# A retention layer feeding a bilinear feed-forward: the opening in another order, w_out in three loads, small TensorE bursts at other places

## The chip, the cores and the metric

The kernel runs on one core of one Trainium2 chip. A core has TensorE (matrix products, into the accumulation memory PSUM), VectorE, ScalarE and GpSimd (elementwise work; GpSimd also issues most loads here), and SyncE, which issues stores and transposing transfers. Each engine takes its own instructions in the order in which the program gives them. Sixteen DMA engines move data between the chip's memory and the on-chip buffer. The metric is the device time of one execution in microseconds (us); the time of a kernel is the median of its runs.

## The reference

Eight batches, eight heads, 576 positions, head size 64. First an attention without softmax, whose scores decay with distance by a factor per head; then a feed-forward whose two inner products are multiplied with each other:

```python
scores = (1 / sqrt(64)) * q @ k.T                       # per batch and head
gamma  = 1 - 2.0 ** (-5 - head)
ret    = scores * where(row >= col, gamma ** (row - col), 0)
x      = (ret @ v), heads side by side                  # 4608 tokens x 512
out    = ((x @ w_a) * (x @ w_b)) @ w_out                # 512 -> 1536 -> 512
```

Inputs and output are float32; the kernel computes in bf16 with float32 sums.

## The kernel before, in words

**Attention in chunks.** The decay is split into a factor on v and k's side (a table `vs`, by position) and one on the output side (a table `qs`), so that the scores need only a triangular mask. A chunk is 128 tokens, a step 64; a running state (the sum of k·v over the steps so far) replaces the scores with earlier steps. `load` (loads of q, k and v, cast to bf16 for q and k, issued by GpSimd), `vscale` (v times its table), `transposes` (q and k of a chunk turned by TensorE, or by a transposing transfer from SyncE), `kv` (the step sums, TensorE, with the additions on VectorE and the bf16 copies of the states on ScalarE put into a list `later`), `stage1` (products with states, then scores, then the masks on VectorE) and `stage2` (scores times v, the rest of the state products, and the writing of x, transposed, by VectorE) handle chunks; a unit is two chunks. Chunks 0 to 3 are taken as two "fresh" units, 0 and 1, of 256 tokens each, by functions of their own (`fresh_...`). These work with one running sum, `kv_sum`.

**Feed-forward in blocks.** A block is 512 tokens. `ffn_ab` makes, for each of 12 columns F of 128, four products with w_a (`pa`), a copy to bf16 by ScalarE (`ha`), four products with w_b (`pb`), and the product of both by VectorE (`hT`). `ffn_out` makes the output of 128 tokens at a time in 12 products with w_out (`po`), copied out by ScalarE and VectorE in turn and stored by SyncE. Both are generators: after each product they yield its cost in units of one 512-column product and whether other work may be put in there. `pop()` at their edges runs one entry of `later`.

**What sets the order.** Every engine's order is written out by hand. The opening is straight code: idle products that keep TensorE going while the first loads come, then the fresh units mixed with the first three columns of block 0. After it, `run` walks the generators and adds up the cost in `at`; the list `todo` holds (position, function, arguments), and at the first edge at or past a position the function is called, so that its instructions stand there in each engine's order. Block 0's columns 3 to 11 take positions 24 to 96, its output 96 to 144; block 1's two halves 144 to 192 and 192 to 240, its output 240 to 288; each later block 144. `first(g)` is `flush` (all of `later`) and `stage1` of unit g; for g from 2 on it also calls the transposing transfers and `vscale` of unit g+2 and the loads of unit g+3. `second(g)` is `flush`, `stage2`, and for g from 2 on `kv` of unit g+2.

**PSUM.** Eight banks in three pools: `ps_ffn` (tag "ab", 4 banks; `pa`, `pb`, `po`, `kv_sum` and some transposes), `ps_o` (2 banks; attention outputs), `ps_x` (2 banks; scores and step sums).

**Loads.** GpSimd issues them in the program's order: unit 0, unit 1, w_a and w_b in pieces by columns (`load_w`, two transfers for each of the two), then all of w_out in one transfer (`load_wo`, line 124), then chunks 4 to 9. Between w_b's columns up to 384 and w_a's from 384 on, GpSimd scales v of unit 1 (`fresh_vscale`, line 479).

The lines that the profile names most: `pa` 414, `ha` 419, `pb` 422, `hT` 427, `po` 453, its copies 462 and 464; transposes 275 and their copies 277 and 278; step sums 294; state products 339, scores 359, masks 367, scores times v 381, x 398; loads of q and k 102, v 110, w_a and w_b 118; `qs` pieces 235. In the opening: idle products 596, transposes 492, copies of the turned q and k 614 to 630, scores 549, masks 561, k·v sums 514 and their bf16 copies 521, state products 527, scores times v 572, x 583 to 588, and 601, `settled`, one small product that reads the last state before the last products of a unit are begun (the probe).

Of the kernel before, what the change touches and what calls it, by code (L numbers as in the profile page):

```python
# [18 lines left out]
def kernel(  # L19
# [240 lines left out]
            op=ALU.mult)  # L260
        vb_of[i] = vb

    def transposes(i, by_dma):
# [8 lines left out]
        tp = ps_ffn.tile([128, 2, HP, 128], BF16, tag="ab", name="tp")  # L272
        for w in (0, 1):
            for p in range(HP):
                nc.tensor.transpose(tp[:, w, p, :],  # L275
                                    qk[:, w, p * 128:(p + 1) * 128], identity)
        nc.scalar.copy(qkT[:, 0], tp[:, 0])
        nc.vector.tensor_copy(qkT[:, 1], tp[:, 1])
# [126 lines left out]
    def ffn_ab(blk, tok0, n, f0, f1):  # L405
# [4 lines left out]
        for F in range(f0, f1):  # L410
# [18 lines left out]
            pop()  # L429
            yield n / 512, True  # L430

    def ffn_out(blk):
        hT = hT_of.pop(blk)
        for u in range(4):
            tok = 512 * blk + 128 * u
            if tok + 128 == NTOK:
                for c0, w, eng, copy in (
                        (0, 320, nc.sync, nc.vector.tensor_copy),
                        (320, 192, nc.scalar, nc.scalar.copy)):
                    pl = ps_ffn.tile([128, 512], FP32, tag="ab", name="po")  # L440
                    for F in range(NF):
                        nc.tensor.matmul(pl[:, 0:w],  # L442
                                         hT[:, F, u * 128:(u + 1) * 128],
                                         wo_sb[:, F, c0:c0 + w],
                                         start=(F == 0), stop=(F == NF - 1))
                        yield w / 512, False
                    osb = o_pool.tile([128, DM], FP32, tag="osb", name="osb")
                    copy(osb[:, 0:w], pl[:, 0:w])
                    eng.dma_start(out[tok:tok + 128, c0:c0 + w], osb[:, 0:w])
                continue  # L450
            po = ps_ffn.tile([128, 512], FP32, tag="ab", name="po")
            for F in range(NF):
                nc.tensor.matmul(po, hT[:, F, u * 128:(u + 1) * 128],  # L453
                                 wo_sb[:, F, :],
                                 start=(F == 0), stop=(F == NF - 1))
# [4 lines left out]
            osb = o_pool.tile([128, DM], FP32, tag="osb", name="osb")  # L460
            if u % 2 == 0:
                nc.scalar.copy(osb, po)  # L462
            else:
                nc.vector.tensor_copy(osb, po)  # L464
            nc.sync.dma_start(out[tok:tok + 128, :], osb)
# [5 lines left out]
    fresh_state = {0: zero_state}  # L471
    fv, fT, fo, fsT = {}, {}, {}, {}

    def fresh_vscale(u, h0, h1, eng):
        if u not in fv:
            fv[u] = [vb_pool.tile([128, DM], BF16, tag="vb", name="fvb")
                     for _ in (0, 1)]
        for e in (0, 1):
            eng.tensor_tensor(  # L479
                fv[u][e].rearrange("p (h d) -> p h d", h=H)[:, h0:h1, :],  # L480
                vf2[:, u, :].rearrange("p (h e d) -> p h e d", h=H, e=2)[
                    :, h0:h1, e, :],
                vs_all[:, 2 * e + u, h0:h1].unsqueeze(2).to_broadcast(
                    [128, h1 - h0, D]), op=ALU.mult)
# [47 lines left out]
    def fresh_state1(u):  # L532
# [2 lines left out]
                 for s in (0, 1)]  # L535
        for j in (0, 2):
            for h, s in ((j, 1), (j + 4, 1), (j + 1, 0), (j + 5, 0)):
                fresh_from_state(u, h, s, j == 0)

    def fresh_scores(u, places):  # L540
        qT, kT = fT[u]
# [24 lines left out]
    def fresh_stage2(u):  # L566
        for j in (0, 2, 1, 3):
            for e in (0, 1):
                for s in (0, 1):
                    for c in (0, 1):  # L570
# [5 lines left out]
                            start=False, stop=True, skip_group_check=True)  # L576
        for j in (0, 2):
            for h, s in ((j, 0), (j + 4, 0), (j + 1, 1), (j + 5, 1)):
                fresh_from_state(u, h, s, False)
        for s in (0, 1):  # L580
            t0 = 256 * u + 128 * s
            if u == 1:
# [16 lines left out]
    def settled(u, n=1, w=128):  # L599
        for _ in range(n):  # L600
# [13 lines left out]
    nc.vector.tensor_tensor(q_out, tq.rearrange("p c e t -> p c t e"),  # L614
                            qs0.rearrange("p c (t e) -> p c t e", e=2),
                            op=ALU.mult)
    nc.scalar.copy(k_out[:, 0:2], tk[0])
    nc.vector.tensor_copy(k_out[:, 2:4], tk[1])
    make_qs(256, 512)
    idle_products(2)  # L620
    fresh_vscale(0, 4, 8, nc.vector)
    fresh_scores(0, (X, AB))
    fresh_kv(0, 0)
    q_out, k_out = fresh_tiles(1)
    tq = fresh_transposed(1, 0, 0, HP, AB)
    nc.scalar.copy(q_out, tq.rearrange("p c e t -> p c t e"))
    tk = fresh_transposed(1, 1, 0, HP, AB)
    fresh_state1(0)
    fresh_kv(0, 1)
    nc.scalar.copy(k_out, tk)  # L630
    fresh_vscale(1, 0, 8, nc.gpsimd)
    load_w(384, 768)
    ramp(idx[:, 512:S], [[1, S - 512]], 512, 0)
    load_w(768, 1152)
    load_w(1152, DFF)
    settled(0)
    fresh_stage2(0)
    fresh_scores(1, (X, O))
    run_all(ffn_ab(0, 0, 256, 0, 1))
    fresh_kv(1, 0)  # L640
    fresh_state1(1)
    fresh_kv(1, 1)
    state_of[8] = fresh_state[4]
    run_all(ffn_ab(0, 0, 256, 1, 2))
    settled(1)
    fresh_stage2(1)
    run_all(ffn_ab(0, 0, 256, 2, NF1))
    run_all(ffn_ab(0, 256, 256, 0, NF1))
    make_keep()
# [56 lines left out]
    for g in range(3, len(units)):  # L706
# [55 lines left out]
```

## Time and profile before

| | |
|---|---|
| time, median of 11 runs | 336.42 us (335.24 to 340.38) |
| the profiled execution's own time | 336.01 us |
| its span | 334.2 us |
| instructions in it | 8838 |
| VectorE, ScalarE, GpSimd busy | 165.4, 112.5, 143.6 us |
| granted TensorE clock | 1.0 throughout |
| read from and written to the chip's memory | 37.75 MB and 9.44 MB |

The span runs from the first to the last instruction of the profiled execution; the time of a run also has what lies around it. In the rows of a timeline, the first number is the start in us, the second the length; then engine, line, operation and tiles (output <- inputs), the count of instructions merged into the row, and in brackets how long the engine had been idle before it and what ended that. The engine names are PE (TensorE), PEld (its weight loads), DVE (VectorE), ACT (ScalarE), POOL (GpSimd) and SP (SyncE). A row of waits gives who waited for whom, the total, the number of times and the longest. A row of stretches gives the stretch, its length, TensorE's busy time and products, the granted clock, the busy share of the DMA engines and GB/s.

### The profile page before, as it was taken

Reading aid. Unit: us, or ns where it says so; the run is one execution under the profiler, and the core shown is the slowest. Engines: PE = TensorE matmul, PEld = TensorE weight load, DVE = VectorE, ACT = ScalarE, POOL = GpSimd, SP = SyncE. Lnnn points to the kernel's source line nnn. Section 1 sums busy time; section 2 is a strip of 40 time slices with the busy share of each in tenths; the row PEclk is TensorE's granted clock in tenths of the full one; section 3 lists DMA queues with packets and bytes.
Section 4 is the critical chain, followed back from the end, with each engine's and each line's share of the span. In section 5 each row is a group of like instructions: output and inputs, shape, how many; then the busy total and the mean of one; then the engine's idle time right before and its main releaser. Section 6 shows DMA issues by size and latency. Waiting matters only on the chain.

```text
span 334.2 us, 8838 instructions
## 1 busy us (share of the span) xinstructions
PE 323.0 (97%) x3746; PEld 166.6 (50%) x3746; DVE 165.4 (49%) x324; ACT 112.5 (34%) x233; POOL 143.6 (43%) x176
## 2 busy tenths in 40 slices
PE   7889889989999999999999999999999999999995
PEld 3564346868544444445444444454444444444443
DVE  6754346757544555346445644454445534444321
ACT  4737523545143213332332223322323133203321
POOL 8786299698647795308250837072100000000000
PEclk9999999999999999999999999999999999999999
DMA  9999999999999999916999499939900700020002
GB/s 144 201 146 195 212 196 235 184 155 139 193 195 196 126 126 224 168 10 92 108 192 118 78 100 230 101 63 123 196 0 29 132 34 1 13 86 31 2 31 94
DMA packets 116151, 40.94 MB, mean 122 GB/s; under 512 B 102992, under 2 KB 109392, under 8 KB 116112
## 3 DMA queue, kind: packets, MB, share of 16 engines
q0 software_dynamic: 80688, 23.34, 71.6%
q1 hardware_dynamic: 35280, 16.95, 28.4%
q8 instruction: 29, 0.48, 0.6%
q10 hardware_dynamic: 144, 0.10, 0.1%
q14 instruction: 10, 0.08, 0.1%
HBM read 37.75 MB, written 9.44 MB: 141 GB/s over the span
## 4 chain that ended last, share of the span: by engine, by line
PE 85%; DMA 9%; POOL 3%; issue 1%; ACT 1%; DVE 0%; POOLq 0%; ACTq 0%
PE po L453 26%; PE pa L414 25%; PE pb L422 25%; DMA wo_sb<-in_moe_w_out_dram 4%; DMA wa_sb<-in_moe_w_a_dram 2%; PE o L339 2%; PE o L381 2%; DMA fqk<-in_k_dram 2%; PE kv L294 2%; DMA qk<-in_k_dram 1%; PE sc L359 1%; POOL fqk L141 1%; PE po L442 1%; POOL fvb L479 1%; PE tp L275 0%
## 5 line engine op out<-in xcount | busy, mean ns | idle before, releaser
L427 DVE TENSOR_TENSOR hT<-ha,pb 128x512 bf16<-128x512 bf16 (+1 forms) x123 | 76.5, 622 | 100.7 <-PE pb L422 85.6
L414 PE MATMUL pa<-xT,wa_sb 128*128 128x512 bf16 (+1 forms) x492 | 114.0, 354 | 2.2 <-issue 1.6
L422 PE MATMUL pb<-xT,wb_sb 128*128 128x512 bf16 (+1 forms) x492 | 113.5, 353 | 0.0
L419 ACT CAST ha<-pa 128x512 bf16<-128x512 f32 (+1 forms) x123 | 65.6, 533 | 124.7 <-PE pa L414 123.6
L453 PE MATMUL po<-wo_sb,hT 128*128 128x512 bf16 x420 | 95.5, 380 | 0.8 <-DMA wo_sb<-in_moe_w_out_dram 0.8
L422 PEld LDWEIGHTS <-wb_sb 128*128 128x128 bf16 x492 | 48.1, 98 | 45.3 <-issue 0.3
L414 PEld LDWEIGHTS <-wa_sb 128*128 128x128 bf16 x492 | 46.8, 98 | 47.0 <-issue 2.9
L256 POOL TENSOR_TENSOR vb<-vf,vs_all 128x512 bf16<-128x512 f32 x30 | 31.6, 1069 | 78.6 <-PE o L339 44.9
L453 PEld LDWEIGHTS <-hT 128*128 128x128 bf16 x420 | 39.0, 98 | 45.6 <-DMA wo_sb<-in_moe_w_out_dram 1.3
L462 ACT COPY osb<-po 128x512 f32<-128x512 f32 x18 | 10.5, 585 | 74.8 <-PE po L453 74.8
L102 POOL DMA_DIRECT2D qk<-in_q_dram x36 | 31.0, 867 | 6.8 <-DMA wo_sb<-in_moe_w_out_dram 6.2
L110 POOL DMA_DIRECT2D vf<-in_v_dram x36 | 31.9, 888 | 1.4 <-issue 1.1
L102 POOL DMA_DIRECT2D qk<-in_k_dram x36 | 31.2, 875 | 0.6 <-DMA wa_sb<-in_moe_w_a_dram 0.3
L367 DVE TENSOR_TENSOR sT<-sc,keep 128x512 bf16<-128x512 f32 x32 | 20.6, 685 | 12.1 <-PE sc L359 12.1
L398 DVE TENSOR_TENSOR xT<-o,qs 128x512 bf16<-128x512 f32 x32 | 20.6, 685 | 11.8 <-PE o L339 11.7
L307 DVE TENSOR_TENSOR s<-kv,s 128x256 f32<-128x256 f32 x49 | 20.6, 420 | 5.8 <-ACT sbf L317 4.5
L317 ACT CAST sbf<-s 128x256 bf16<-128x256 f32 x56 | 21.1, 406 | 3.1 <-DVE s L305 2.7
L464 DVE COPY osb<-po 128x512 f32<-128x512 f32 x17 | 11.7, 687 | 19.3 <-PE po L453 19.3
L339 PE MATMUL o<-qkT,sbf 64*64 64x64 bf16 x456 | 12.1, 196 | 0.1
L339 PEld LDWEIGHTS <-sbf 64*64 64x64 bf16 x456 | 8.2, 108 | 5.7 <-issue 5.5
L381 PEld LDWEIGHTS <-vb 64*64 64x64 bf16 x512 | 6.4, 108 | 6.6 <-issue 6.6
L381 PE MATMUL o<-sT,vb 64*64 64x64 bf16 x512 | 8.2, 195 | 0.0
(75 smaller groups left out, 128.7 us busy)
## 6 DMA issues: line engine op xcount, KB each, us to landing
out_dram<-osb SPq DMA_DIRECT2D x35, 256.0 KB, 5.1
vf<-in_v_dram POOLq DMA_DIRECT2D x29, 256.0 KB, 6.1
qk<-in_q_dram POOLq DMA_DIRECT2D x28, 128.0 KB, 6.3
qk<-in_k_dram POOLq DMA_DIRECT2D x28, 128.0 KB, 7.0
wo_sb<-in_moe_w_out_dram POOLq DMA_DIRECT2D x1, 1536.0 KB, 14.6
wa_sb<-in_moe_w_a_dram POOLq DMA_DIRECT2D x6, 192.0 KB, 6.5
wb_sb<-in_moe_w_b_dram POOLq DMA_DIRECT2D x6, 192.0 KB, 7.5
vf<-in_v_dram POOLq DMA_DIRECT2D x8, 128.0 KB, 5.9
```

The source lines that it names most:

```text
L102: nc.gpsimd.dma_start(t[r0:r0 + n, w, :].rearrange("p (h d) -> p h d", h=H), src[b, :, s0:s0 + n, :].rearrange("h s d -> s h d"))
L110: nc.gpsimd.dma_start(t[r0:r0 + n, :].rearrange("p (h d) -> p h d", h=H), v[b, :, s0:s0 + n, :].rearrange("h s d -> s h d"))
L256: eng.tensor_tensor(vb.rearrange("p (h d) -> p h d", h=H), vf.rearrange("p (h d) -> p h d", h=H), vs[:, i % PER, :].unsqueeze(2).to_broadc ...
L307: nc.vector.tensor_tensor(new, ps[s][:, ci], last_sum[0], op=ALU.add)
L317: nc.scalar.copy(sb, new)
L339: nc.tensor.matmul(o[s][half(c), ci, j, :], st[half(r), p, :], qkt_of[i][half(r), 0, p, half(s)], start=start, stop=True, skip_group_check ...
L381: nc.tensor.matmul(o[s][half(c), ci, j, :], vb[half(s), 64 * h:64 * h + 64], sT[half(s), h % 2, ci, h // 2, :], start=False, stop=True, sk ...
L414: nc.tensor.matmul(pa[:, 0:n], wa_sb[:, c, fs], xT[:, c, tok0:tok0 + n], start=(c == 0), stop=(c == NC - 1))
L419: nc.scalar.copy(ha[:, 0:n], pa[:, 0:n])
L422: nc.tensor.matmul(pb[:, 0:n], wb_sb[:, c, fs], xT[:, c, tok0:tok0 + n], start=(c == 0), stop=(c == NC - 1))
L427: nc.vector.tensor_tensor(hT[:, F, off:off + n], ha[:, 0:n], pb[:, 0:n], op=ALU.mult)
L453: nc.tensor.matmul(po, hT[:, F, u * 128:(u + 1) * 128], wo_sb[:, F, :], start=(F == 0), stop=(F == NF - 1))
```

## The change

- Unit 0 is carried to its end (states, second k·v sum, last products, x) before k of unit 1 is transposed; before, q and k of unit 1 were transposed in between. Products with the zero state at the beginning of the sequence (8 in all) fall away.
- The copy of unit 1's transposed k is split between ScalarE and VectorE.
- v of unit 1 is scaled on VectorE (even rows, one instruction) and ScalarE (odd rows, one instruction for each head) where GpSimd did both. `load_w(384, 768)` is so right behind its forerunner in GpSimd's order.
- Column 1 of block 0's first half is begun (its four `pa` products) between the two k·v sums of unit 1, and ended after unit 1's last products.
- The four `qs` pieces of unit 1 are put at other places in ScalarE's order.
- w_out comes in three loads of four rows of blocks, with the loads of chunks 4 and 5 between; block 0's output is made in three passes over all four groups of 128 tokens (`ffn_out_parts`), so that each pass needs one third of w_out. Its four stores come in the last pass.
- The transposes of chunks 4 and 5 go to `ps_x`; chunk 4's stand at position 96 (was 112).
- `kv` of units 2 and 3 at 208 and 228 (were 184 and 208), `first` and `second` of unit 2 at 248 and 260 (were 232 and 244), of unit 3 at 272 and 280 (were 260 and 272).

```diff
+    def store(tok, po, u):
...
+    def ffn_out_parts(blk, parts):
+
+        hT = hT_of.pop(blk)
+        po = [ps_ffn.tile([128, 512], FP32, tag="ab", name="po")
+              for _ in range(4)]
+        for f0, f1 in parts:
+            for u in range(4):
+                for F in range(f0, f1):
+                    nc.tensor.matmul(po[u], hT[:, F, u * 128:(u + 1) * 128],
+                                     wo_sb[:, F, :],
+                                     start=(F == 0), stop=(F == NF - 1))
+                    if F < f1 - 1:
+                        yield 1.0, False
+                if f1 == NF:
+                    store(512 * blk + 128 * u, po[u], u)
+                pop()
+                yield 1.0, True
...
-        for e in (0, 1):
+        for e in es:
+            if eng is nc.scalar:
+                for h in range(h0, h1):
+                    nc.scalar.activation(
+                        fv[u][e][:, 64 * h:64 * h + 64],
+                        vf2[:, u, 128 * h + 64 * e:128 * h + 64 * e + 64],
+                        AF.Copy, bias=0.0,
+                        scale=vs_all[:, 2 * e + u, h:h + 1])
+                continue
...
-                fresh_from_state(u, h, s, j == 0)
+                if u or s:
+                    fresh_from_state(u, h, s, j == 0)
...
+    make_qs(256, 512, (0, 1))
     nc.scalar.copy(k_out[:, 0:2], tk[0])
     nc.vector.tensor_copy(k_out[:, 2:4], tk[1])
-    make_qs(256, 512)
+    make_qs(256, 512, (2,))
     idle_products(2)
     fresh_vscale(0, 4, 8, nc.vector)
     fresh_scores(0, (X, AB))
     fresh_kv(0, 0)
+    make_qs(256, 512, (3,))
+    fresh_state1(0)
+    fresh_kv(0, 1)
     q_out, k_out = fresh_tiles(1)
     tq = fresh_transposed(1, 0, 0, HP, AB)
     nc.scalar.copy(q_out, tq.rearrange("p c e t -> p c t e"))
-    tk = fresh_transposed(1, 1, 0, HP, AB)
-    fresh_state1(0)
-    fresh_kv(0, 1)
-    nc.scalar.copy(k_out, tk)
-    fresh_vscale(1, 0, 8, nc.gpsimd)
+    settled(0)
+    fresh_stage2(0)
+    tk = [fresh_transposed(1, 1, 0, 2, AB), fresh_transposed(1, 1, 2, 4, X)]
+    nc.scalar.copy(k_out[:, 0:2], tk[0])
+    nc.vector.tensor_copy(k_out[:, 2:4], tk[1])
     load_w(384, 768)
+    fresh_vscale(1, 0, 8, nc.vector, (0,))
+    fresh_vscale(1, 0, 8, nc.scalar, (1,))
+    fresh_scores(1, (X, O))
+    run_all(ffn_ab(0, 0, 256, 0, 1))
+    fresh_kv(1, 0)
+    begun = ffn_ab(0, 0, 256, 1, 2)
+    for _ in range(NC):
+        next(begun)
+    fresh_state1(1)
+    fresh_kv(1, 1)
+    state_of[8] = fresh_state[4]
     ramp(idx[:, 512:S], [[1, S - 512]], 512, 0)
     load_w(768, 1152)
     load_w(1152, DFF)
-    settled(0)
-    fresh_stage2(0)
-    fresh_scores(1, (X, O))
-    run_all(ffn_ab(0, 0, 256, 0, 1))
-    fresh_kv(1, 0)
-    fresh_state1(1)
-    fresh_kv(1, 1)
-    state_of[8] = fresh_state[4]
-    run_all(ffn_ab(0, 0, 256, 1, 2))
     settled(1)
     fresh_stage2(1)
+    run_all(begun)
     run_all(ffn_ab(0, 0, 256, 2, NF1))
...
-    load_wo(0, NF)
...
-    load(*range(4, 10))
-    todo = [(110, vscale, (4, nc.vector)), (110, vscale, (5, nc.vector)),
-            (110, transposes, (4, False)), (112, transposes, (5, False)),
-            (116, kv, (units[0], nc.scalar)),
+    PARTS = ((0, 4), (4, 8), (8, NF))
+    load_wo(*PARTS[0])
+    load(4)
+    load_wo(*PARTS[1])
+    load(5)
+    load_wo(*PARTS[2])
+    load(*range(6, 10))
+    todo = [(90, vscale, (4, nc.vector)),
+            (90, transposes, (4, False, ps_x, "x")),
+            (108, vscale, (5, nc.vector)),
+            (112, transposes, (5, False, ps_x, "x")),
+            (117, kv, (units[0], nc.scalar)),
             (128, first, (0,)), (136, second, (0,)),
...
-            (184, kv, (units[2], nc.scalar)),
+            (208, kv, (units[2], nc.scalar)),
...
-            (207, kv, (units[3], nc.scalar)),
-            (232, first, (2,)), (244, second, (2,))]
+            (226, kv, (units[3], nc.scalar)),
+            (247, first, (2,)), (257, second, (2,)),
+            (271, first, (3,)), (278, second, (3,))]
...
-    run(ffn_out(0))
+    run(ffn_out_parts(0, PARTS))
```

More of the change, by code (lines that the diff above doesn't have):

```diff
@@ L261, in vscale, with transposes @@
         vb_of[i] = vb
-    def transposes(i, by_dma):
+    def transposes(i, by_dma, place=ps_ffn, tag="ab"):
         qk = qk_of[i]
@@ L271, in transposes @@
             return
-        tp = ps_ffn.tile([128, 2, HP, 128], BF16, tag="ab", name="tp")
+        tp = place.tile([128, 2, HP, 128], BF16, tag=tag, name="tp")
         for w in (0, 1):
@@ L430, in ffn_ab @@
             yield n / 512, True
+    def store(tok, po, u):
+        osb = o_pool.tile([128, DM], FP32, tag="osb", name="osb")
+        if u % 2 == 0:
+            nc.scalar.copy(osb, po)
+        else:
+            nc.vector.tensor_copy(osb, po)
+        nc.sync.dma_start(out[tok:tok + 128, :], osb)
+    def ffn_out_parts(blk, parts):
[14 more added lines that the diff above has]
+                yield 1.0, True
     def ffn_out(blk):
@@ L459, in ffn_out @@
                     yield 1.0, F % 4 == 3
[L460 to L465, printed above, removed]
+            store(tok, po, u)
             pop()
@@ L470, with fresh_vscale @@
     kv_sum = ps_ffn.tile([128, 512], FP32, tag="ab", name="kv_sum")
-    fresh_state = {0: zero_state}
+    fresh_state = {}
     fv, fT, fo, fsT = {}, {}, {}, {}
-    def fresh_vscale(u, h0, h1, eng):
+    def fresh_vscale(u, h0, h1, eng, es=(0, 1)):
         if u not in fv:
@@ L575, in fresh_stage2 @@
                             fsT[u][e][half(s), h % 2, h // 2, :],
-                            start=False, stop=True, skip_group_check=True)
+                            start=(u == 0 and s == 0 and j == 0 and e == 0),
+                            stop=True, skip_group_check=True)
         for j in (0, 2):
             for h, s in ((j, 0), (j + 4, 0), (j + 1, 1), (j + 5, 1)):
-                fresh_from_state(u, h, s, False)
+                if u or s:
+                    fresh_from_state(u, h, s, False)
         for s in (0, 1):
@@ L705 @@
                  (68 + 4 * j, make_qs, (0, 256, (j,)))]
-    for g in range(3, len(units)):
+    for g in range(4, len(units)):
         p = 288 + 144 * ((units[g][0] - 8) // 4)
```

## The prediction

> **What bounds the kernel now.** I read four views, in this order: busy shares, what TensorE waited for, the stretches, and the timeline around each wait.
>
> ```profile
> PE 323.0 (97%) x3746; PEld 166.6 (50%) x3746; DVE 165.4 (49%) x324; ACT 112.5 (34%) x233; POOL 143.6 (43%) x176
> ```
>
> TensorE is busy 323.0 of the 334.2 us span. Only the other 11.2 us can be won without removing products. The waits of TensorE say which of it:
>
> ```profile
> PE pa L414 <- issue: 1.6, 1, 1.6
> PE tp L275 <- DMA qk<-in_k_dram: 1.1, 1, 1.1
> PE po L453 <- DMA wo_sb<-in_moe_w_out_dram: 0.8, 1, 0.8
> ...
> PE kv_sum L601 <- ACT sbf L521: 0.5, 1, 0.5
> PE fo L527 <- ACT sbf L521: 0.5, 1, 0.5
> PE pa L414 <- DVE xT L583: 0.4, 1, 0.4
> ```
>
> The stretches of TensorE show that nothing is left to win late; this row is full, and so are those after it up to 330 us:
>
> ```profile
> 95.00:130.00 35.00, 35.00 (x398) 1.00 1.35 169
> ```
>
> So the case is decided in the first 95 us. The timeline there (start, length, engine, line, work, idle time before it):
>
> ```profile
> 14.69 2.05 POOL L479 TENSOR_TENSOR fvb<-vf,vs_all 128x512 bf16<-128x512 f32 x2
> 16.68 1.26 POOL L118 DMA_DIRECT2D wa_sb<-in_moe_w_a_dram  x2
> ...
> 25.89 1.04 POOL L124 DMA_DIRECT2D wo_sb<-in_moe_w_out_dram  x1 [0.37 <-DMA wa_sb<-in_moe_w_a_dram]
> ...
> 40.49 3.63 PE L453 MATMUL po<-wo_sb,hT 128*128 128x512 bf16 x16 [0.85 <-DMA wo_sb<-in_moe_w_out_dram]
> 40.74 0.88 POOL L102 DMA_DIRECT2D qk<-in_q_dram  x1 [6.25 <-DMA wo_sb<-in_moe_w_out_dram]
> ...
> 46.08 0.40 PE L275 MATMUL tp<-identity,qk 128*128 128x128 bf16 x4 [1.12 <-DMA qk<-in_k_dram]
> ...
> 66.50 0.44 PE L294 MATMUL kv<-vb,qk 64*64 64x64 bf16 x24
> 66.87 0.50 PE L414 MATMUL pa<-xT,wa_sb 128*128 128x256 bf16 x3
> 69.02 0.28 PE L414 MATMUL pa<-xT,wa_sb 128*128 128x256 bf16 x1 [1.64 <-issue]
> ```
>
> Read it so. GpSimd scales unit 1's v for 2.05 us, and the next w_a load stands behind that in its queue until 16.68. One DMA brings all of w_out; it lands at 40.44, 0.85 us too late. Each GpSimd DMA waits until the one eight before it has landed (in the built program it waits on the semaphore that the eighth last used), so q of chunk 5 is held 6.25 us by w_out, and TensorE then waits 1.12 us for chunk 5's k. At 67.38, in the middle of four like products, TensorE waits 1.64 us for nothing that the trace names.
>
> **The change part by part.** I count positions as the kernel's list does: one 512-column product is 1, and 0.216 us.
>
> *Opening.* Up to the end of unit 0's first k·v sum (10.62) TensorE's order is the old one. The two exps now ahead of ScalarE's k copy take 1.0 us of the 1.78 us that it idled before 8.21: nothing lost. Then, by hand, with 0.05 us from one engine to the next (the state copy that ends at 13.11 and the probe that starts at 13.16 show it) and the old durations: state copy 10.67 to 11.03 (L521, 0.37); second k·v sum to 11.55; its copy to 11.97, behind the last exp; q transposes to 12.1. Unit 0's last product waits for the fourth mask, which ends at 12.65 as before, so it ends at 13.1 (was 14.05). ScalarE now runs without a gap: q copy 1.01, x copy 0.59, half the k copy 0.58, from 12.16 to 14.34. Unit 1's scores start at 14.40 (were split, 14.08 and 14.73), and its masks, behind 0.69 us of DVE scaling, end at 17.5 (17.2).
>
> Then ScalarE scales half of v in 8 pieces of 128x64. No row is that operation. The nearest are these two (mean ns is the number after the comma):
>
> ```profile
> L235 ACT ACTIVATE qs<-idx,biasq,lgp 128x64 f32<-128x64 f32 x4 | 1.5, 435 | 0.0
> L200 ACT ACTIVATE vs_all<-vs_all 128x72 f32<-128x72 f32 x1 | 0.3, 263 | 1.6 <-DVE vs_all L196 1.6
> ```
>
> The first has the size, but reads scale and bias from memory; two in a row take 0.77 us, so 0.335 each and 0.435 for the last: 8 make 2.78 us. [...] I take 2.0. ScalarE is then free at 16.35, k·v of unit 1 ends at 16.8, its copy at 17.23, states and the second sum at 17.8, the copy at 18.2, the probe and the last product at 19.1, and x of unit 1 (2 x 0.645) at 20.45, which TensorE needed at 21.32. Meanwhile it has the rest of block F1 and all of F2, 1.3 us, from 19.05 to 20.35. Gain 0.8 us; with 2.78 instead it is 0.05, and with 0.435 apiece end to end (3.5 us) a loss of 0.7. Eight zero products fall away (0.1 us, inside this). I book 0.75.
>
> *w_out in thirds.* The 2.05 us now gone from GpSimd bring w_a's third load from 16.68 to about 14.7. From there on the transfers are the limit: equal weight pieces land about 1.05 us apart (the GpSimd issues held at 24.91, 25.89, 27.86 and 28.84 date them). So the stream runs 2.0 us ahead, and w_out in one piece would land at 38.4. It took some 7 us behind the last weights, 2.3 per third, and chunks 4 and 5 took 5.6 us (40.44 to 46.03). In the new order: first third 33.7, chunk 4 36.5, second third 38.9, chunk 5 41.7, last third 44.0. TensorE, 0.75 us ahead, reaches chunk 4's transposes at 38.9, the second third and chunk 5 at 42.8 (16 x 0.216 and 0.45 later), the last third at 47.0. All are there, the closest by 1.1 us: 0.85 + 1.12 = 1.97 us gained. Two more issues of 1.04 us on GpSimd fall into the 6.25 us that it idled. Chunk 6 and later follow about 3 us sooner. The four outputs of block 0 leave in a burst from 132 to 144; behind them on SP stand only the transposes of chunks 8 and 9, needed at 248. All four banks of the output sums are held together, and the transposes use the other pool, free by then.
>
> *Bursts elsewhere.* In the 3.7 us ahead of the stall at 67.38 stand states, scores and outputs of unit 1 and k·v of unit 2, 120 small products, with few wide ones between. By the count of the built program the stalled weight load is TensorE's 1,715th instruction; an odd 0.41 us hole in weight loading at 15.74 is before its 447th. The page has a queue for code:
>
> ```profile
> q8 instruction: 29, 0.48, 0.6%
> ```
>
> 16 KB each. [...] I book the whole 1.64; the ends are 0 and 1.64, and a stall of its own elsewhere.
>
> *Against it.* From 260 to 272 VectorE must copy the output, write x and add three k·v sums (0.69 + 1.29 + 1.25, from 0.7 after 260): 3.95 us, where TensorE comes for their bank after 3.7. A wait of 0.25. Position 280 leaves 8 products, 1.73 us, for x of unit 3, 1.4 us of work: none.
>
> Sum: -0.75 - 0.85 - 1.12 - 1.64 + 0.25 = -4.1 us. The profiled execution took 336.01 us (334.2 span and 1.8 around it) and would take 331.9. The median shown is 336.42, 0.4 above it; the stalls are the same program's, so I take 336.42 - 4.1 = 332.3. About 0.3% (1 us) is what can be told from no change.
>
> **The rivals.**
> (a) The code stall stays, or comes at another dense place, since its cause is argued from two holes: 332.3 + 1.6 = 333.9. Against it: 80 to 84 us had as dense a stretch and no stall.
> (b) ScalarE's pieces cost 2.78 to 3.5 us: 333.0 to 333.8. For it: the row of the same size; against it: one operand less.
> (c) The thirds don't come in time, that is, the change doesn't do what it says: w_out's end moves behind chunk 4 and 5 and TensorE waits at 128 instead, for up to the 2 us gained: 334.3. With (a) and (b) as well, 336.5, no change.
> (d) Slower: chunk 4's transposes stand in TensorE's order ahead of the whole output product. Its six pieces took 10.9 us to land with all of w_out ahead. If they share the engines with the thirds and chunk 5, and end with them at 44.0, TensorE stands 5.1 us from 38.9: 332.3 + 5.1 = 337.4. From a landing at 43.0 nothing is left of the gain, from 44.0 the kernel is slower by 0.3%. Against it: pieces landed in order of issue.
>
> **How the numbers follow.** All steps as booked 0.54, (a) 0.19, (b) 0.10, (c) 0.09, (d) 0.08. The likeliest gives 332.3. Its own range is 331.5 to 333.0 (opening 0.05 to 1.0, the wait 0 to 0.5). The range with (a), (b) and most of (c) is 331.3 to 335.0. Faster than 335.4: the first three and most of (c), 0.86; within 0.3%: the rest of (c) and the low end of (d), 0.06; slower 0.08.
>
> **What would show it.** The first product on unit 1's tokens at about 20.5 (was 21.32); no wait of TensorE on w_out or on a chunk's k; chunk 4's transposes at 38.9; the first w_a load after 14.07 at 14.7; no 1.6 us of "issue" before 95 us; block 2 starting near 90.9 (94.9 before). A wait on q, k or w_out between 38 and 48 us, or "issue" of a microsecond anywhere, would make it wrong.

## The result and the profile after

The changed kernel took 334.08 us (330.78 to 338.83) beside 336.23 us for the kernel before; the ratio is 0.9903, 95% interval 0.9877 to 0.9929. The predicted 332.3 us lies 1.8 us under this median. Two later sets of the same kernel, told below, gave 331.15 and 331.97 us; over all three the median is 332.1. The profiled execution took 331.98 us with a span of 330.2; that of before had 336.01 and 334.2. So the two traces differ by 4.0 us, and that is what they can account for. Executions more than 1.5% above the fastest of their kernel are left out of all ratios and of the medians by clock below; without them, and with the profiled execution, the first set's median is 333.1 us, near what its ratio says (3.3 us less than before).

The busy shares of the page after:

```profile
PE 322.1 (98%) x3738; PEld 166.5 (50%) x3738; DVE 166.0 (50%) x326; ACT 114.1 (35%) x241; POOL 143.0 (43%) x176
```

TensorE's busy time is smaller by 0.9 us, and the rest of the 4.0 us was waiting. What TensorE waited for after the change:

```profile
PE kv_sum L628 <- DVE idle L174: 1.2, 1, 1.2
PE o L339 <- issue: 1.2, 1, 1.2
PE ftp L521 <- DMA fqk<-in_q_dram: 0.8, 1, 0.8
PE fsc L579 <- ACT fT L666: 0.5, 1, 0.5
PE fo L556 <- ACT sbf L550: 0.5, 1, 0.5
PE kv_sum L633 <- ACT sbf L550: 0.5, 1, 0.5
```

The waits for w_out, for a chunk's k and for unit 1's x are not in it any more, nor is the stall of 1.6 us in front of a product with w_a. In its place stands one that is new: 1.2 us of "issue" ahead of a state product. The timeline shows where (start, length, engine, line, work, idle time before it):

```profile
14.01 2.02 ACT L502 ACTIVATE fvb<-vf,vs_all 128x64 bf16<-128x64 f32 x8
...
20.17 0.61 PE L414 MATMUL pa<-xT,wa_sb 128*128 128x256 bf16 x4
...
22.80 1.03 PE L414 MATMUL pa<-xT,wa_sb 128*128 128x512 bf16 x4
...
45.74 0.88 POOL L102 DMA_DIRECT2D qk<-in_q_dram  x1 [1.50 <-DMA wo_sb<-in_moe_w_out_dram]
...
51.29 0.61 PE L275 MATMUL tp<-identity,qk 128*128 128x128 bf16 x8
...
84.61 0.61 PE L359 MATMUL sc<-qkT 64*64 64x64 bf16 x32
...
87.32 0.20 PE L339 MATMUL o<-qkT,sbf 64*64 64x64 bf16 x2
88.67 0.25 PE L339 MATMUL o<-qkT,sbf 64*64 64x64 bf16 x6 [1.15 <-issue]
...
90.91 1.02 PE L414 MATMUL pa<-xT,wa_sb 128*128 128x512 bf16 x4
```

The same points in the kernel before (rows of two views; the second ended at 95 us, which cuts its last row short):

```profile
21.32 0.60 PE L414 MATMUL pa<-xT,wa_sb 128*128 128x256 bf16 x4 [0.40 <-DVE xT L583]
...
23.93 1.03 PE L414 MATMUL pa<-xT,wa_sb 128*128 128x512 bf16 x4
...
55.21 0.61 PE L275 MATMUL tp<-identity,qk 128*128 128x128 bf16 x8
...
87.51 0.43 PE L359 MATMUL sc<-qkT 64*64 64x64 bf16 x32
...
94.91 0.38 PE L414 MATMUL pa<-xT,wa_sb 128*128 128x512 bf16 x1
```

ScalarE's eight pieces take 2.02 us. The first product on unit 1's tokens starts at 20.17 (21.32 before). GpSimd's row at 45.74 had been held by the last third of w_out, which by its semaphore landed at 45.2 where the prediction had 44.0; TensorE needs it at 47.2. The other landings came out within 0.7 us of the prediction's (33.6, 35.8, 38.4 and 41.1). Block 2 starts at 90.91 (94.91 before).

Two stretches, the output of block 0 and the time up to block 2 (length; busy time of TensorE, its weight loads, VectorE, ScalarE and GpSimd, each with its count; granted clock, DMA share, GB/s):

```profile
38.90:47.00 8.10, 8.10 (x101) 3.92 (x101) 3.63 (x8) 2.39 (x5) 6.55 (x9) 1.00 1.50 178
64.00:91.00 27.00, 25.85 (x454) 17.46 (x453) 15.52 (x35) 10.37 (x26) 22.29 (x26) 1.00 1.58 179
```

The first is full, which says that the thirds arrive in time. The second lacks just the 1.15 us of issue.

Like points of the two traces, with the difference that each stretch made (at position 240, which is no one product, small products that stand on different sides of it are allowed for):

| point | before | after | of this stretch | booked |
|---|---|---|---|---|
| column 3 of block 0, first 512-column product | 23.93 | 22.80 | -1.13 | -0.75 |
| transposes of chunk 6 | 55.21 | 51.29 | -2.79 | -1.97 |
| position 240, ahead of unit 2's first stage | | | -1.66 | -1.64 |
| block 2 | 94.91 | 90.91 | +1.58 | +0.25 |

### The profile page after: what moved, and what is told of

Its sections match the earlier page's. It is cut to its first block, busy times and chain, and to the rows that moved or that the text cites. A ratio compares the mean times of both kernels' runs of the same rounds, so it can differ in the third digit from the quotient of the medians.

```text
span 330.2 us, 8833 instructions
## 1 busy us (share of the span) xinstructions
PE 322.1 (98%) x3738; PEld 166.5 (50%) x3738; DVE 166.0 (50%) x326; ACT 114.1 (35%) x241; POOL 143.0 (43%) x176
## 4 chain that ended last, share of the span: by engine, by line
PE 96%; DMA 1%; ACT 1%; issue 1%; ACTq 0%; POOLq 0%
PE pa L414 29%; PE pb L422 28%; PE po L479 25%; PE po L448 3%; PE o L339 2%; PE o L381 2%; PE kv L294 2%; DMA fqk<-in_q_dram 1%; PE sc L359 1%; PE ftp L521 1%; PE po L468 1%; PE tp L275 1%; PE kv_sum L628 0%; PE fsc L579 0%; PE kv_sum L543 0%
## 5 line engine op out<-in xcount | busy, mean ns | idle before, releaser
L479 PEld LDWEIGHTS <-hT 128*128 128x128 bf16 x372 | 34.5, 98 | 39.4
```

The costliest lines, as they stand in the source:

```text
L479: nc.tensor.matmul(po, hT[:, F, u * 128:(u + 1) * 128], wo_sb[:, F, :], start=(F == 0), stop=(F == NF - 1))
```

## The experiments

**Each part alone.** The first three kernels add one part each to the kernel before, which took 336.37 us beside them.

The opening alone:

```diff
+    make_qs(256, 512, (0, 1))
...
+    make_qs(256, 512, (3,))
+    fresh_state1(0)
+    fresh_kv(0, 1)
...
-    fresh_vscale(1, 0, 8, nc.gpsimd)
...
+    load_w(384, 768)
+    fresh_vscale(1, 0, 8, nc.vector, (0,))
+    fresh_vscale(1, 0, 8, nc.scalar, (1,))
```

> The kernel before with the new opening alone (w_out in one load, old places of the small products). Theory (waits): block 0's column 3 starts 1.1 us sooner; the weights stream 2 us sooner, so the 0.85 us wait on w_out goes; chunk 5's q is still held by w_out's landing, so TensorE still waits about 1 us on chunk 5's k; the 1.6 us code hole stays near 65 us. Sum -2.0 us, 334.2. Rival (the opening's gain is swallowed by the wait on w_out, which is set by the transfers alone): under 0.3 us, 336.

Measured: 334.34 us, ratio 0.9931 (0.9903 to 0.9958). Its waits:

```profile
PE pa L414 <- issue: 1.8, 1, 1.8
...
PE tp L275 <- DMA qk<-in_k_dram: 1.0, 1, 1.0
...
PE pb L422 <- DMA wb_sb<-in_moe_w_b_dram: 0.6, 1, 0.6
```

The opening does two things. TensorE gets through it 1.2 us sooner (column 3 starts at 22.76), and the wait for w_out is gone though w_out still comes in one load: GpSimd's order, freed of 2 us of scaling, brings it sooner. The wait for chunk 5's k stays, and so does the stall of issue at its old place. New is a wait for w_b.

w_out in thirds alone:

```diff
-    load(*range(4, 10))
+    load_wo(*PARTS[0])
+    load(4)
+    load_wo(*PARTS[1])
+    load(5)
+    load_wo(*PARTS[2])
+    load(*range(6, 10))
...
-    run(ffn_out(0))
+    run(ffn_out_parts(0, PARTS))
```

> The kernel before with w_out in thirds, block 0's output in three passes and chunk 4 and 5 at their new places; old opening, old places of the other small products. Theory: no wait on w_out; chunk 5's k lands at about 43.7 where TensorE comes at 43.4, so a wait of at most 0.5 is left: -2.0 to -2.6 us, 334. Rival (without GpSimd freed in the opening the thirds come too late): a wait of 1 to 2 us on the last third or on chunk 4, 336 or more.

Measured: 335.47 us, ratio 0.9960 (0.9922 to 0.9997). Its waits:

```profile
PE pa L414 <- issue: 2.1, 1, 2.1
...
PE kv L294 <- DMA qk<-in_k_dram: 0.9, 1, 0.9
...
PE o L339 <- issue: 0.6, 1, 0.6
```

Neither w_out nor chunk 5's k is waited for, without the new opening's help. But three holes further on grew or are new: the stall of issue is 2.1 us in place of 1.6, and at 88 to 91 us stand 0.6 us of issue and 0.9 us for the k of chunk 15. What the thirds gain is in part given back there.

The bursts alone:

```diff
-            (184, kv, (units[2], nc.scalar)),
+            (208, kv, (units[2], nc.scalar)),
...
-            (207, kv, (units[3], nc.scalar)),
-            (232, first, (2,)), (244, second, (2,))]
+            (226, kv, (units[3], nc.scalar)),
+            (247, first, (2,)), (257, second, (2,)),
+            (271, first, (3,)), (278, second, (3,))]
```

> The kernel before with only the new places of the small products of units 2 and 3. Theory (code comes in blocks of 256 instructions, and a block that runs faster than the next one arrives stalls): no hole near TensorE's 1,715th instruction (67 us), but one of about 1 us at or near its 2,481st, 766 later; -0.3 to -0.8 us, 335.6. Rival (the hole at 67 us has to do with the data of that column): it stays there, 336.2 or above.

Measured: 334.97 us, ratio 0.9958 (0.9937 to 0.9979). The gain of 1.4 us is larger than expected: the trace has no stall of issue of 0.3 us or more at all, neither at the old place nor at 2,481. The rest of this trace doesn't compare, because in its opening TensorE was granted half its clock:

```profile
12.00:14.00 2.00, 1.53 (x59) 0.72 1.61 187
14.00:22.00 8.00, 7.28 (x129) 0.50 0.99 132
22.00:24.00 2.00, 1.95 (x40) 0.72 1.18 170
```

(The number behind the count of products is the granted clock.) The three ratios multiply to 0.985; the changed kernel's three sets gave 0.9903, 0.9847 and 0.9872. The parts add up within what can be measured.

**The scaling on GpSimd again**, in the changed kernel:

```diff
+    fresh_vscale(1, 0, 8, nc.gpsimd)
     load_w(384, 768)
-    fresh_vscale(1, 0, 8, nc.vector, (0,))
-    fresh_vscale(1, 0, 8, nc.scalar, (1,))
```

> The changed kernel with v of unit 1 scaled on GpSimd again, ahead of w_a's third load. Theory (GpSimd's order holds the whole stream): the third w_a load at about 16.6 instead of 14.54, every later load 2 us later, block 0's column 3 0.5 us later, and a wait of TensorE of 0.5 to 1.5 us on chunk 5's k or the second third: +1 to +2 us against the changed kernel. Rival (the stream has slack there): only the 0.5 us.

Measured: 334.89 us, ratio 0.9933 (0.9901 to 0.9966).

```profile
PE kv L294 <- DMA qk<-in_k_dram: 2.8, 1, 2.8
...
PE kv_sum L543 <- POOL fvb L508: 0.7, 1, 0.7
```

The wait of 0.7 us for GpSimd's scaling is there as expected. The 2 us that all later transfers lose don't show at w_out, which the thirds cover, but at 89 us, where TensorE waits 2.8 us for k of chunk 15. The trace is of an execution that took 336.82 us and in which the clock fell twice, so its 2.8 us is no size to build on, and the median lies near that of the changed kernel's first set. The gain of moving the scaling is not told apart here from what one kernel's sets differ by.

**The changed kernel again**, to learn why 334.08 is not 332.

> The changed kernel again, beside the kernels below. Theory (clock): its executions fall into two groups, near 331.9 us where the mean granted clock is 0.998 or more, and 1.5 to 3 us longer where it is less, because no wait is left that would take up a slower opening; the median stands near 333.5 to 334.1. Rival (code): the spread comes from stalls like the 1.15 us at 87.5 us and not from the clock; then the times don't follow the clock.

Measured: 331.15 us, ratio 0.9847 (0.9781 to 0.9913); and, in another set beside the last kernels of this section,

> The changed kernel once more, as the measure for the two below. Theory (its two medians so far, 334.08 and 331.15, are draws from the same wide distribution): a median between the two, and single executions from 330.6 to 335. Rival (the first set was the odd one): a median near 331.5 again.

331.97 us, ratio 0.9872 (0.9832 to 0.9913). The high median was not repeated. In the first set 7 of 12 executions had a mean granted clock under 0.998, in the two later ones 2 of 10. Over the three sets, the 13 executions at 0.998 or more have a median of 331.9 us and the 9 with less have 334.3. In the kernel before, over its four sets beside these runs, it is 336.2 (43 executions) and 337.0 (39). A lower clock goes with 2.4 us more in the changed kernel and 0.9 in the kernel before. (A later expectation has 2.5 and 1.0.) That these two figures differ is not shown by so few executions: when the executions are drawn again at random, their difference comes out anywhere from -0.7 to 2.6 us. The clock is not all, either: one execution at 0.993 took 331.15.

**The opening filled.**

```diff
+    idle_products(2, 256)
...
     make_qs(256, 512, (3,))
+    fill(3)
     fresh_state1(0)
...
+    fill(3)
     fresh_scores(1, (X, O))
...
+    fill(3)
     settled(1)
```

> The changed kernel with idle products of 0.33 us in three of TensorE's waits in the opening (ahead of unit 0's first state products, of unit 1's scores and of unit 1's last product), and 2 more of 256 columns at the start. Theory that an emptier TensorE in the opening lets the clock drop: more executions at a clock of 0.998 or more, and a median 0.5 to 1.5 us below the changed kernel's. Rival (the clock drops for reasons of its own): the same shares, and the same median or up to 0.5 us more, since the products can come in the way of the work that waited.

Measured: 331.81 us, beside 331.15 for the changed kernel. All six executions had a clock of 0.999 or 1.0, but so had, at 0.998 or more, the six of the next kernel, which fills nothing. No gain is shown, and the medians don't tell what lowers the clock; what stood ahead of its falls in the traces is in the last section.

**Does slack explain the clock's price?** The kernel before, its opening made 1.5 us longer:

```diff
     settled(1)
+    idle_products(7)
     fresh_stage2(1)
```

> The kernel before with 7 idle products of 512 columns (1.5 us) ahead of unit 1's last product, so that its opening ends 1.5 us later. Theory (the waits for w_out and for chunk 5's k, 1.97 us together, take up what the opening loses, which is why a lower clock there costs the kernel before 1.0 us and the changed kernel 2.5): the first product on unit 1's tokens at 22.8, no wait for w_out, 0.5 us or less for chunk 5's k, block 2 starting near 94.9 as before, and a median within 0.4 us of the kernel before. Rival (the transfers follow TensorE, so that both waits stay): 1.5 us slower.

Measured: 337.20 us beside 336.89; ratio 0.9999 (0.9967 to 1.0031), so 1.5 us, 0.45%, is excluded. Its timeline:

```profile
22.58 0.60 PE L414 MATMUL pa<-xT,wa_sb 128*128 128x256 bf16 x4 [0.40 <-DVE xT L583]
...
40.73 3.62 PE L453 MATMUL po<-wo_sb,hT 128*128 128x512 bf16 x16
...
45.30 0.40 PE L275 MATMUL tp<-identity,qk 128*128 128x128 bf16 x4 [0.28 <-DMA qk<-in_k_dram]
```

TensorE is 1.3 us later at 22.58, finds w_out there, and waits 0.28 us for chunk 5's k in place of 1.12: two transfers that nobody waits for in the changed kernel gave the kernel before room for 1.5 us. Block 2 starts at 95.45 (94.91 before), behind a longer stall of issue (2.05 us, below) and a new wait of 0.79 us for k of chunk 15. Whether this room also makes a lower clock cheaper is not shown: no trace of the changed kernel itself has a lower clock.

**The code blocks.** The kernel before, with 32 more instructions at the start, nearly the same columns:

```diff
-    idle_products(9)
+    idle_products(7)
+    idle_products(18, 64)
```

> The kernel before, with 2 of the 9 idle products of 512 columns at the start made into 18 of 64 columns: 16 more products, 32 more instructions, nearly the same columns. Theory (blocks of 256 counted from the start): the stall that stood ahead of weight load 1,715 stands 32 instructions earlier in the code, ahead of about number 1,683 of the old count, within the products k.v of unit 2 or just at their end, and is at least as long, 1.5 to 3 us, as the block before it then runs in 3.6 us in place of 5.3. Rival (it belongs to that column or to a missing wait there): it stays in the column's four products with w_a behind unit 2's k.v.

```profile
66.38 0.34 PE L294 MATMUL kv<-vb,qk 64*64 64x64 bf16 x11
67.71 0.31 PE L294 MATMUL kv<-vb,qk 64*64 64x64 bf16 x13 [0.98 <-issue]
67.95 0.61 PE L414 MATMUL pa<-xT,wa_sb 128*128 128x256 bf16 x4
```

Measured: 335.41 us in a single execution, so the trace is the result here. The stall stands ahead of weight load 1,715 of this kernel's own count, that is, 32 instructions earlier in the code: now within the products k·v. Only its length, 0.98 us, is below what was expected. The kernel with the longer opening, which has 14 instructions more, shows the same thing unasked: its stall, 2.05 us, is ahead of its own number 1,715, in k·v too. The stalls by number (TensorE's weight loads and products counted together; the view puts the one at 1,717 down to ScalarE):

| kernel | number | what stands there | us |
|---|---|---|---|
| before | 1,715 | product with w_a | 1.64 |
| opening alone | 1,715; 2,481 | product with w_a; k·v | 1.8; 0.3 |
| thirds alone | 1,715; 2,481 | product with w_a; state product | 2.1; 0.6 |
| 32 more at the start | 1,715 | k·v of unit 2 | 0.98 |
| longer opening | 1,715 | k·v of unit 2 | 2.05 |
| changed, three traces | 2,481 | state product | 1.15; 0.23; 0.59 |
| opening filled | 447; 1,717 | product with w_a | 0.66; 0.44 |

1,715 and 2,481 lie 766 apart. With TensorE's waits counted too, as the traces of before and after record them, number 2,481 is the 2,498th record in both; in that of before 1,715 is the 1,730th and 447, with the hole of 0.41 us in weight loading ahead of it, the 450th. These lie 768 and 1,280 apart, three and five times 256. The stall belongs to a number, not to a place. Its length is not fixed: with the code unchanged up to number 2,481 it was 1.15, 0.23 and 0.59 us in three executions, and none in a fourth (k·v of unit 5 later, below).

The traces also hold the transfers of the code itself. Queue q8 of the page moves 29 packets of 16 KB. At 256 instructions each that is 7,424; the trace of before has 7,525 records of TensorE, waits counted, and 506 or fewer of any other engine. The views only add these packets up; the trace has the start and end of each. Beside the stalls (us):

| kernel | number | packet moves | TensorE goes on | after the packet's end |
|---|---|---|---|---|
| before | 1,715 | 66.43 to 67.53 | 69.01 | 1.5 |
| opening alone | 1,715 | 65.30 to 66.26 | 67.66 | 1.4 |
| thirds alone | 1,715 | 63.77 to 64.81 | 66.44 | 1.6 |
| 32 more at the start | 1,715 | 64.96 to 66.31 | 67.71 | 1.4 |
| longer opening | 1,715 | 65.41 to 66.76 | 68.14 | 1.4 |
| changed, first set | 2,481 | 86.42 to 87.30 | 88.67 | 1.4 |
| changed, third set | 2,481 | 86.02 to 86.96 | 88.41 | 1.5 |
| changed, second set | 2,481 | 85.07 to 86.29 | 87.74 | 1.4 |
| k·v of unit 5 later | 2,481 | 84.52 to 85.45 | 87.78, no stall | 2.3 |

In all 14 stalls, those of the kernels not in this table and the small holes at 447 among them, TensorE goes on 1.3 to 1.6 us after its packet is in. That points to the late supply of code as the cause, with a stall as long as its packet was late. How fast the block before runs is only half of it. At 1,715 that block took 3.0 to 4.0 us in the five traces with the old bursts, which all stalled, and 5.2 us or more in the nine with the new ones, of which one stalled for 0.44 us. At 2,481 a block of 5.9 us stalled in three traces and not in three others, and one of 7.4 us still stalled in the kernels with the opening and with the thirds alone. The other half is when the packet starts. In the changed kernel's first trace it started at most 1.1 us after TensorE had begun the block before where no other transfer ran in between, and up to 5.0 us after it where loads ran. That the loads hold it up is likely, but no run changes them alone.

**Room ahead of number 2,481.**

```diff
-            (247, first, (2,)), (257, second, (2,)),
+            (238, first, (2,)), (248, second, (2,)),
```

> The changed kernel with the first and second stage of unit 2 nine positions earlier (238 and 248), so that 9 more wide products stand in the 256 instructions ahead of number 2,481, which then take about 7.6 us in place of 5.7. Theory (code comes in blocks of 256, and a block that runs out before the next has come leaves TensorE standing): no stall of issue at 87 to 88 us, span 329.0, median 0.5 to 1.1 us below the changed kernel's. Rival (the stall belongs to that place in the code): a stall of about 1 us stays with unit 3's second stage, and the time is the same.

Measured: 332.59 us beside 331.15. No stall at 2,481, but a new wait:

```profile
77.18 0.22 PE L359 MATMUL sc<-qkT 64*64 64x64 bf16 x2 [0.67 <-DVE s L307]
77.64 0.44 PE L359 MATMUL sc<-qkT 64*64 64x64 bf16 x30 [0.24 <-DVE s L307]
```

The scores of unit 2 now come before VectorE has added the sums of unit 3's k·v, which hold the bank. What was won at 88 us is lost at 77, and block 2 starts at 90.91 again. The missing stall is no test of the longer block, for the code packet was in at 85.97, which by estimate would just have done for the old order too: 1.4 us later is 87.4, and the changed kernel's first trace had TensorE there at 87.5.

**k·v of unit 5 later.** In the changed kernel's trace of the second set, block 2 was held by k:

```profile
88.86 0.32 PE L294 MATMUL kv<-vb,qk 64*64 64x64 bf16 x16 [0.68 <-DMA qk<-in_k_dram]
```

With the code stall at 0.23 us TensorE comes to chunk 15's k too soon, and block 2 starts at 90.85. Two late things stand in line in this execution; in the first set's that k had landed at 86.95, and nothing stood behind the stall.

```diff
-        if 4 <= g + 2 < len(units):
+        if 4 <= g + 2 < len(units) and g != 3:
...
-            (271, first, (3,)), (278, second, (3,))]
+            (271, first, (3,)), (278, second, (3,)),
+            (296, kv, (units[5], nc.scalar))]
```

> The changed kernel with the k.v sums of unit 5 taken out of the second stage of unit 3 (position 278) and put at position 296, inside block 2. Theory (two late things stand one behind the other ahead of block 2: the code block before weight load 2,481 and the k of chunk 15): where the code stall is short, 0.7 us are gained, where it is long nothing; block 2 starts at 90.2 to 90.7, the median 0 to 0.7 us below the changed kernel's. Rival (the wait for k is only moved): block 2 starts 1.3 us earlier and the same wait stands in it; same time.

```profile
87.80 0.24 PE L339 MATMUL o<-qkT,sbf 64*64 64x64 bf16 x8
87.97 1.90 PE L479 MATMUL po<-wo_sb,hT 128*128 128x512 bf16 x8
89.71 1.03 PE L414 MATMUL pa<-xT,wa_sb 128*128 128x512 bf16 x4
90.57 1.03 PE L422 MATMUL pb<-xT,wb_sb 128*128 128x512 bf16 x4
91.53 0.45 PE L294 MATMUL kv<-vb,qk 64*64 64x64 bf16 x32
91.91 1.04 PE L414 MATMUL pa<-xT,wa_sb 128*128 128x512 bf16 x4
```

Measured: 331.87 us, beside 331.97 for the changed kernel. In this execution neither hole is there, but the edit is not shown to have removed them: the code packet was in at 85.45 (86.9 with 1.4 us behind it) and k landed at 86.36, by estimate early enough for the unchanged order, in whose first trace TensorE came to number 2,481 at 87.5. The products at 91.91 stand at 92.38 in the changed kernel's trace of the same set: 0.5 us in one trace, nothing that the medians can show.

With unit 2's stages at 238 and 248 and k·v of unit 3 at 221 as well:

> The changed kernel with both: stages of unit 2 at 238 and 248, k.v of unit 3 at 221 in place of 226 so that its sums free their bank before the scores of unit 2, and k.v of unit 5 at 296. Theory: neither the code stall nor the wait for chunk 15's k nor the 0.9 us ahead of unit 2's scores; block 2 starts near 89.7 and the median is 1.0 to 1.3 us below the changed kernel's. Rival (the transfers or another engine set this stretch, and every hole removed comes back elsewhere): block 2 starts at 90.9 once more, and the median is the same within 0.3%.

Measured: 333.07 us, ratio 0.9913 (0.9886 to 0.9939).

```profile
PE sc L359 <- DVE s L307: 0.9, 2, 0.7
...
PE kv L294 <- DVE s L307: 0.6, 1, 0.6
```

The wait ahead of the scores stays in full and the moved k·v waits 0.6 us of its own for a bank. Block 2 starts at 91.25, and the median is 1.1 us above the changed kernel's of the same set. The sums on VectorE set this stretch, by their place in its order and not by its load: from 72.9 to 74.5 VectorE stands 1.58 us for a product of the feed-forward that is ahead of them. None of the variants beats the changed kernel.

## Why the prediction was right, and where its steps were not

**The whole.** 4.1 us were booked against the profiled execution, and the profiled pair differs by 4.0. The first set shows 2.2 us by its medians and 3.3 by its ratio; the later sets show 5.2 and 4.4 by their medians. The weak step is the last one, in which a difference of one profiled pair was taken off the median: half of the changed kernel's executions lie within 2.5 us (331.4 to 333.9), half of the kernel before's within 1.7 (335.6 to 337.3), so one small set of it says little. The waits that were removed had also been room, since the kernel before takes 1.5 us more in its opening without being longer; that this made the first set long is not shown. In part the sum is luck, as the stretches below show. The prediction named "issue" of a microsecond anywhere as a sign of being wrong, and 1.15 us of it stand at 88 us. (In its chances, the first three paths make 0.83, so the 0.86 holds a third of (c) and not most of it.)

**The opening.** Booked 0.75, measured 1.13. The disputed term was ScalarE's pieces. No row of before and no run ahead of the result shows the 2.0 us that was taken for them; the trace after has 2.02 us for the eight, the nearest row's 2.78 was not right, and rival (b) falls. The rest of the difference is mostly that the pieces began at 14.01 where the prediction had 14.34. The wait for w_b in the products ahead of unit 1's first k·v was not foreseen. It was 0.6 and 0.9 us in two later traces of the changed kernel, whose first product on unit 1's tokens came at 20.16 and 20.48, and 1.1 us in the kernel with k·v of unit 5 later, whose opening is the same, with 20.65: up to 0.5 us of it reached the end of the opening.

**w_out in thirds.** Both waits are gone, and the stretch gained 2.79 us where 1.97 were booked. The sizes of the waits were the wrong ones to add up. A view counts a wait from the end of the last product, but in an unbroken run the next product starts before that end: a row of four products lasts 1.03 us, and the next row starts 0.86 us after it. In start times the two waits cost 1.02 and 1.28 us. Another 0.18 us was a wait of chunk 4 and 5's transposes for q, and 0.27 one of the first state products of chunks 4 and 5 for their states; the rows of before hide them, since rows of small products overlap. The landing of the last third was estimated 1.2 us too soon, and the margin of 3 us bore it. Rivals (c) and (d) didn't come: chunk 4's transposes stood at 38.34.

**Code.** Here the step failed in part. The stall at 1,715 went as booked, with its 1.64 us. That size is a row of before; that the small products ahead of it bring the stall about, and that moving them takes it away, was the author's estimate, which no run had shown. The bursts alone then had no stall of 0.3 us or more. What was not worked out is the bursts' new place: 766 further on, the 256 instructions ahead of number 2,481 took 7.4 us before and 5.9 after, and 1.15 us came back there in the profiled execution, which is rival (a)'s "another dense place". What was booked as free of stalls has one of 0 to 1.15 us, from execution to execution. In the profiled one it cost its full length, since k of chunk 15, next in line, had landed at 86.95; in the second set's that k landed at 88.82 and would have held TensorE anyway.

**The new wait.** Booked 0.25. There is no stall, but the scores at 84.61 last 0.61 us where an undisturbed row of 32 takes 0.43: 0.18 us. With the 1.15 us, which cost 1.31 in start times, that is all but 0.1 of the 1.58 us that this stretch lost.

So the sum was right with two errors that cancel: the first two stretches gained 1.2 us more than booked, the last lost 1.3 us more.

## What to carry to other kernels

A wait that is removed had also been room for whatever came late before it (here for 1.5 us in the opening), so measure several sets before a median is believed. Price a wait by the start times of the products around it, since its listed size leaves out the overlap that is lost (here 0.85 and 1.12 us listed, 1.02 and 1.28 in start times). Where a stall has no releaser, count the engine's instructions. Here it moved with the count when 32 were added at the start, and the trace's own code packets, which were in 1.3 to 1.6 us before TensorE went on, told how late the code was. Thinning out the 256 instructions ahead of 1,715 took its stall away in eight of nine traces and left 0.44 us in one; so count again where the small bursts are moved to. Before they are moved, look at who frees the bank that they write, since VectorE's sums stood right behind.

## What the runs showed of the hardware that was not expected

**Code.** Each trace has 29 packets of code of 16 KB; in that of before, 7,525 records of TensorE make 259 for each, and numbers 447, 1,715 and 2,481, which follow holes in this trace or in others, stand 1,280 and 768 records apart, whole multiples of 256. In all 14 stalls TensorE went on 1.3 to 1.6 us after a packet was in. It stood 0.23 to 1.15 us at the same number of the same kernel, and 0.98 to 2.1 us at number 1,715 of the kernels with the old bursts. At most two of a trace's 29 packets had a stall behind them.

**The clock.** In the kernel with the bursts alone TensorE had 0.50 of its clock from 12.89 to 23.13 us; in that with the scaling on GpSimd from 7.44 to 10.85 and from 92.77 to 96.19. These changes lie 10.24 us apart in the one, and 3.41, 81.92 and 3.41 us in the other; in the traces of before and after, the first and the last record of the clock lie 324.27 and 320.85 us apart. All are whole multiples of 3.41 us. TensorE's busy time in stretches of that length, counted from a change on (in the thirds alone, which has no fall, from the first record of its clock on):

| stretch | busy us | clock in the next stretch |
|---|---|---|
| bursts alone, 9.48 to 12.89 | 1.76 | falls to 0.50 |
| scaling on GpSimd, 4.03 to 7.44 | 1.64 | falls to 0.50 |
| scaling on GpSimd, 89.36 to 92.77 (the wait of 2.8 us) | 0.92 | falls to 0.50 |
| thirds alone, 62.49 to 65.90 (the stall of 2.1 us) | 1.81 | stays 1.00 |
| bursts alone, 12.89 to 16.30 and 16.30 to 19.72, at 0.50 | 3.05, 2.95 | stays 0.50 |
| bursts alone, 19.72 to 23.13, at 0.50 | 3.41 | back to 1.00 |
| scaling on GpSimd, 7.44 to 10.85 and 92.77 to 96.19, at 0.50 | 3.41, 3.41 | back to 1.00 |

Over all 14 traces, counted so from the first record of the clock on, these three are the stretches with the least work, and the 1.81 us is the least that went without a fall. In these traces the clock fell after stretches with 0.92, 1.64 and 1.76 us of work and came back after three without a hole (3.41 us of work). Three falls are few, and that such stretches are what the clock follows is the author's reading, which no run shows. The first record of the clock lies at 4.03 to 10.04 us, so the stretches begin at other instructions in each execution; whether the same holes leave the clock alone in one execution and not in the next for that reason is not shown. By estimate, a stretch at half clock takes 0.005 off the mean of an execution of 332 us (half of 3.41 over 332) and costs at most 1.7 us of TensorE's time. The listed clocks crowd near 0.995 and 0.990, as one or two such stretches would make them.
